# Sliding-window attention and a SwiGLU block on one core: wide half tiles, key spreading on two engines, and another order of the first phase

## The chip, the core and the metric

The kernel runs on one core of a Trainium2 chip. The metric is the device time of one execution in microseconds (us). A profiled execution also gives a span, from its first to its last instruction, which is shorter (in before 405.4 us where the execution took 407.19). PE is TensorE (matmuls), PEld its weight loads, DVE is VectorE, ACT is ScalarE, POOL is GpSimd, and SP is the engine whose queue issues the loads and stores here. A trailing q (SPq, POOLq) means the queue of that engine. One execution of e10 fell into a slower state (584.02 us at a granted clock of 0.643, against 0.959 to 0.966 in its other runs); all comparisons below are of runs in the fast state.

## The reference

```python
# q, k, v: (8 batches, 8 heads, 576 positions, 64)
scores = q @ k.T / 8, kept where 0 <= query position - key position < 64
attn   = softmax(scores)
x      = (attn @ v) laid out as 4608 tokens x 512
out    = (silu(x @ w_gate) * (x @ w_val)) @ w_out      # 512 -> 1536 -> 512
```

## The kernel before

Attention is done in groups of 128 tokens, inputs come in blocks of 256 tokens (number n), and the feed-forward part works on tiles of 512 tokens (number t). All of it is one program: a first phase fills the pipeline, then a loop over groups 8 to 35 mixes attention of later groups with feed-forward of earlier ones. In the timelines below an engine's instructions start in the order in which the program gives them: in the changed kernel ScalarE's query copy starts at 24.32 us, after the key copies that stand ahead of it, though TensorE had turned the queries by 21.0.

Keys of a block are transposed on TensorE into one PSUM tile `tp`, and spread from there into a block-diagonal SBUF tile. Queries are transposed and copied by ScalarE:

```python
    def turn_k(n):
        tp = turned(n, "k_f")                 # 8 transposes into one PSUM tile
        for a in range(2):                    # a: half of the partitions
            for c in range(2):                # c: even or odd keys
                y = 64 * a + c
                dve.tensor_copy(
                    kbd[n % KR][64 * a:64 * a + 64, :, :, y:y + 63:2],
                    tp[64 * a:64 * a + 64, c].rearrange("r p (i x) -> r p i x", x=32),
                )

    def turn_q(n):
        tp = turned(n, "q_f")
        act.copy(qT[n % QR][:], tp[:])
```

The feed-forward step `gv` computes gate and value for one block of 128 channels, over `n` columns from `c0`. In the first phase, where only half a tile of tokens is ready, it takes 256 columns:

```python
        for ps, w in ((g_ps, wg), (v_ps, wv)):
            for c in range(4):
                nc.tensor.matmul(
                    ps[:, 0:n], w[:, c, P * m:P * m + P], xT[t][:, c, c0:c0 + n],
                    start=(c == 0), stop=(c == 3),
                )
        act.activation(th[:, 0:n], g_ps[:, 0:n], AF.Tanh, scale=0.5)
# gate:   sg = (th + 1) * g_ps        value: hT = sg * v_ps        (both on VectorE)
```

`mix(xs, ys)` issues the feed-forward steps xs and deals the attention steps ys out between them. The end of the first phase:

```python
    mix(O(0, (2, 3)), [lambda: products(9), lambda: scores(11, pool), lambda: turn_x(9)])
    casts_all(6, pool, act)
    mix(F(1, range(8, 12), 256, 256),
        [lambda: products(10), lambda: turn_k(6), lambda: turn_q(6), lambda: turn_x(10),
         lambda: scores(12, pool)])
    load(8, k, "k_f", sp)
    load(8, q, "q_f", sp)
    casts(7, "k_f", pool)
    # ... cut: products, scores and turns of the last groups before the loop
    for w in range(8, NG):                    # the loop
        ...
```

The softmax here doesn't subtract the row's maximum and nothing guards it: scores larger than these inputs give would overflow.

## Time and profile before

| | before |
|---|---|
| time, median of 3 runs | 407.66 us (406.01 to 408.82) |
| span of the profiled run | 405.4 us |
| first gate matmul | 20.2 us |
| start of the loop (its first gate matmul) | 117.4 us |
| from there to the end of the span | 288.0 us |
| PE busy from 117.4 to 386.0 | 266.7 of 268.6 us |

The page's digits show in which slices an engine is busy. A table by stage says how full each engine is in a stretch of time, and the list of waits says what a given engine stood for. The lines are in the prediction below. What they say is short: the loop is bound by TensorE and has no waits; the first 117 us have 27.5 us of holes on TensorE, so that is where a change can win.

### The profile page before, as it was taken

To read this page: it belongs to the slowest core of one execution; us is meant where nothing else is said; L and a number is where in the kernel's file an instruction comes from. 1 tells how busy PE (TensorE), PEld (TensorE's weight loads), DVE (VectorE), ACT (ScalarE), POOL (GpSimd) and SP (SyncE) were. 2 spreads that over 40 slices of the span, in tenths; PEclk is the share of its full clock that TensorE was granted. 3 is DMA by queue.
4 is the path that set the end of the run, shared out by engine and by line. 5 is a ranking of instruction groups with operands and counts; after the bars stand their busy time and mean duration, and the time that the engine had idled before them with its cause. 6 is when DMAs were issued, how large, how long until landed. Compare 5 with 4: busy or idle time off the path is not lost.

```text
span 405.4 us, 7092 instructions
## 1 busy us (share of the span) xinstructions
PE 357.0 (88%) x2617; PEld 211.8 (52%) x2656; DVE 248.5 (61%) x511; ACT 170.4 (42%) x307; POOL 152.4 (38%) x194
## 2 busy tenths in 40 slices
PE   2596898989779999999999999999999999999910
PEld 1474657675655555555555555555555554444400
DVE  6777988756667675747576676767676544554100
ACT  3353545363653545344444445343535434322200
POOL 4542333463574445554444445554443420000000
PEclk9998999999989999999999999999999999999975
DMA  9999897036442444434443434444432100111111
GB/s 190 237 220 228 162 199 169 3 119 163 134 105 62 113 108 111 112 106 108 107 112 107 106 108 112 120 124 114 114 76 57 35 32 27 31 39 36 36 52 44
DMA packets 87411, 42.94 MB, mean 106 GB/s; under 512 B 40272, under 2 KB 82768, under 8 KB 87376
## 3 DMA queue, kind: packets, MB, share of 16 engines
q1 hardware_dynamic: 81552, 37.76, 36.5%
q0 software_dynamic: 5824, 4.72, 7.3%
q8 instruction: 21, 0.34, 0.3%
q14 instruction: 14, 0.11, 0.1%
HBM read 37.75 MB, written 9.44 MB: 116 GB/s over the span
## 4 chain that ended last, share of the span: by engine, by line
PE 78%; DVE 8%; DMA 3%; ACT 3%; issue 2%; POOL 1%; SPq 0%; DVEq 0%; ACTq 0%; POOLq 0%
PE g_ps L251 22%; PE v_ps L251 22%; PE o_ps L276 21%; PE ao_ps L220 5%; PE tp L129 4%; DMA out_dram<-os__5021 2%; PE xtp L236 2%; DVE kbd_93 L137 2%; PE s_ps L189 2%; DVE kbd_95 L137 1%; DVE x_b L225 1%; DMA k_f<-in_k_dram 1%; DVE sg L262 1%; DVE hT L267 1%; PE s_ps L182 1%
## 5 line engine op out<-in xcount | busy, mean ns | idle before, releaser
L262 DVE SCALAR_TENSOR_TENSOR sg<-th,g_ps 128x512 f32<-128x512 f32 (+1 forms) x126 | 76.7, 609 | 76.4 <-ACT th L256 74.9
L251 PE MATMUL g_ps<-xT,wg 128*128 128x512 bf16 (+1 forms) x487 | 114.3, 353 | 5.7 <-DVE sg L262 3.0
L251 PE MATMUL v_ps<-xT,wv 128*128 128x512 bf16 (+1 forms) x500 | 115.2, 352 | 0.5
L256 ACT ACTIVATE th<-g_ps 128x512 f32<-128x512 f32 (+1 forms) x126 | 67.9, 539 | 110.1 <-PE g_ps L251 95.4
L276 PE MATMUL o_ps<-wo,hT 128*128 128x512 bf16 x414 | 96.0, 379 | 0.6
L267 DVE TENSOR_TENSOR hT<-sg,v_ps 128x512 bf16<-128x512 f32 (+1 forms) x126 | 76.8, 610 | 11.4 <-PE ao_ps L220 0.5
L251 PEld LDWEIGHTS <-wv 128*128 128x128 bf16 x504 | 50.0, 99 | 45.2
L251 PEld LDWEIGHTS <-wg 128*128 128x128 bf16 x504 | 47.2, 100 | 38.6 <-issue 6.2
L276 PEld LDWEIGHTS <-hT 128*128 128x128 bf16 x432 | 41.2, 98 | 44.6
L225 DVE TENSOR_TENSOR x_b<-ao_ps,r 128x256 bf16<-128x256 f32 x72 | 30.6, 425 | 2.5
L192 POOL TENSOR_TENSOR E_104<-E_104,mask 128x512 bf16<-128x512 bf16 (+1 forms) x16 | 17.6, 1123 | 33.2 <-ACT E_104 L191 29.7
L192 POOL TENSOR_TENSOR E_102<-E_102,mask 128x512 bf16<-128x512 bf16 (+2 forms) x18 | 17.0, 964 | 27.9 <-ACT E_102 L191 27.9
L192 POOL TENSOR_TENSOR E_105<-E_105,mask 128x512 bf16<-128x512 bf16 x16 | 18.1, 1152 | 23.1 <-ACT E_105 L191 23.1
L238 ACT COPY xT<-xtp 128x512 bf16<-128x512 bf16 x36 | 21.3, 591 | 12.8 <-PE xtp L236 12.8
L137 DVE COPY kbd_94<-tp 64x512 bf16<-64x512 bf16 x24 | 16.0, 716 | 11.5 <-PE tp L129 11.4
L137 DVE COPY kbd_95<-tp 64x512 bf16<-64x512 bf16 x24 | 16.0, 715 | 9.9 <-PE tp L129 9.8
L137 DVE COPY kbd_93<-tp 64x512 bf16<-64x512 bf16 x24 | 16.0, 716 | 8.6 <-PE tp L129 8.5
L192 POOL TENSOR_TENSOR E_103<-E_103,mask 128x512 bf16<-128x512 bf16 x14 | 15.8, 1155 | 11.4 <-ACT E_103 L191 11.4
L129 PE MATMUL tp<-identb,k_fb 128*128 128x128 bf16 x144 | 12.3, 234 | 6.9 <-DVE k_fb L100 6.7
L236 PE MATMUL xtp<-identb,x_b 128*128 128x128 bf16 x144 | 14.9, 226 | 1.9 <-DVE x_b L225 1.4
L100 POOL CAST k_fb<-k_f 128x1024 bf16<-128x1024 f32 x15 | 15.5, 1036 | 0.7
L129 PEld LDWEIGHTS <-k_fb 128*128 128x128 bf16 x144 | 10.5, 106 | 9.3 <-DVE k_fb L100 6.7
(148 smaller groups left out, 422.7 us busy)
## 6 DMA issues: line engine op xcount, KB each, us to landing
v_f<-in_v_dram SPq DMA_DIRECT2D x144, 64.0 KB
k_f<-in_k_dram SPq DMA_DIRECT2D x12, 512.0 KB
q_f<-in_q_dram SPq DMA_DIRECT2D x12, 512.0 KB
wg<-in_moe_w_gate_dram POOLq DMA_DIRECT2D x4, 384.0 KB, 6.9
wv<-in_moe_w_val_dram POOLq DMA_DIRECT2D x4, 384.0 KB, 8.8
k_f<-in_k_dram SPq DMA_DIRECT2D x4, 384.0 KB
q_f<-in_q_dram SPq DMA_DIRECT2D x4, 384.0 KB
wo<-in_moe_w_out_dram POOLq DMA_DIRECT2D x4, 384.0 KB, 10.1
```

What stands on the lines that cost most here:

```text
L129: nc.tensor.transpose(tp[:, c, p, :], x_b[:, c, P * p:P * p + P], identb[:])
L137: dve.tensor_copy(kbd[n % KR][64 * a:64 * a + 64, :, :, y:y + 63:2], tp[64 * a:64 * a + 64, c].rearrange("r p (i x) -> r p i x", x=32),)
L192: eng.tensor_mul(e, e, mask[:, lo:hi, :].unsqueeze(1).to_broadcast([P, 2, hi - lo, 64]))
L220: nc.tensor.matmul(o_ps[:, i, :], w, x, start=(n == 0), stop=(n == len(parts) - 1))
L225: dve.tensor_mul(x_b[:, 256 * h:256 * h + 256].rearrange("r (p a d) -> r p a d", p=2, a=2), o_ps[:, :, 0:P].rearrange("r p (a d) -> r p a ...
L236: nc.tensor.transpose(tp[:, p, :], x_b[:, P * p:P * p + P], identb[:])
L238: act.copy(xT[g // 4][:, :, off:off + P], tp[:])
L251: nc.tensor.matmul(ps[:, 0:n], w[:, c, P * m:P * m + P], xT[t][:, c, c0:c0 + n], start=(c == 0), stop=(c == 3),)
L256: act.activation(th[:, 0:n], g_ps[:, 0:n], AF.Tanh, scale=0.5)
L262: dve.scalar_tensor_tensor(sg[:, 0:n], th[:, 0:n], 1.0, g_ps[:, 0:n], ALU.add, ALU.mult)
L267: dve.tensor_mul(hT[t][:, m, c0:c0 + n], sg[:, 0:n], v_ps[:, 0:n])
L276: nc.tensor.matmul(o_ps[:], hT[t][:, c, P * s:P * s + P], wo[:, c, :], start=(c == 0), stop=(c == 11),)
```

## The change

The intent: elementwise work on half tiles takes more than half the time of a full tile (the step for `sg` in before: 416 ns at 256 columns, 686 at 512), so a half tile takes two channel blocks at once and stays 512 wide. VectorE was busy in the holes, so half of the key copies go to ScalarE and many clears to GpSimd. The first phase gets an order in which attention and feed-forward alternate more evenly. Weights come in other slices.

```diff
     def turn_k(n):
         tp = turned(n, "k_f")
-        for a in range(2):
-            for c in range(2):
+        for c in range(2):
+            for a, copy in ((0, dve.tensor_copy), (1, act.copy)):
                 y = 64 * a + c
-                dve.tensor_copy(
+                copy(
                     kbd[n % KR][64 * a:64 * a + 64, :, :, y:y + 63:2],
                     tp[64 * a:64 * a + 64, c].rearrange("r p (i x) -> r p i x", x=32),
                 )
@@ gv: a half tile takes channel blocks m and m + 1
+            for i in range(1 if half is None else 2):
+                o, n, x = (0, 512, 0) if half is None else (256 * i, 256, 256 * half)
+                for c in range(4):
+                    nc.tensor.matmul(
+                        ps[:, o:o + n], w[:, c, P * (m + i):P * (m + i) + P],
+                        xT[t][:, c, x:x + n], start=(c == 0), stop=(c == 3),
+                    )
@@ clears: half of each buffer, values on GpSimd, ahead of their use
+    def clear(i):
+        for a in range(2):
+            ...
+            dve.memset(kbd[i][h, :, :, z:z + 64], 0.0)
+            for vb in vbd[2 * i:2 * i + 2]:
+                pool.memset(vb[h, :, :, z:z + 64], 0.0)
+                ...
@@ inputs of the last blocks
+    def next_inputs(n):
+        casts_all(n, pool, act)
+        load(n + 1, k, "k_f", sp)
+        load(n + 1, q, "q_f", sp)
+        load_v(2 * n + 2)
+        load_v(2 * n + 3)
+
+    def last_inputs():
+        casts(7, "k_f", pool)
+        casts(7, "q_f", act)
+        load(8, k, "k_f", sp)
+        load(8, q, "q_f", sp)
@@ order (cut to its last mixture)
+    mix(F(0, range(8, 12)) + F(1, (0, 2, 4, 6), 1) + O(0, (0, 1)) + F(1, (8, 9)) + O(0, (2, 3))
+        + F(1, (10, 11)), att3[5:] + [
+            lambda: turn_k(4), lambda: turn_q(4), lambda: scores(8, pool, 1, 4),
+            lambda: next_inputs(5), lambda: scores(9, pool), lambda: products(8),
+            lambda: turn_x(8), lambda: turn_k(5), lambda: turn_q(5), lambda: scores(10, pool),
+            lambda: next_inputs(6), lambda: products(9), lambda: scores(11, pool),
+            lambda: turn_x(9), lambda: turn_k(6), lambda: products(10), lambda: turn_q(6),
+            lambda: turn_x(10), lambda: scores(12, pool), last_inputs, lambda: products(11),
+            lambda: scores(13, pool), lambda: turn_x(11), lambda: turn_k(7), lambda: turn_q(7)])
```

More of the change, by code (lines that the diff above doesn't have):

```diff
@@ L152, in queries, with weights_gv @@
         return x[:, m % 4:m % 4 + n]
-    def weights_gv(s):
+    def weights_gv(m0, m1):
         for dst, src in ((wg, moe_w_gate), (wv, moe_w_val)):
             pool.dma_start(
-                dst[:, :, 384 * s:384 * s + 384],
-                src[:, 384 * s:384 * s + 384].rearrange("(c r) f -> r c f", r=P),
+                dst[:, :, P * m0:P * m1],
+                src[:, P * m0:P * m1].rearrange("(c r) f -> r c f", r=P),
             )
@@ L162, in weights_o @@
         pool.dma_start(
-            wo[:, 3 * s:3 * s + 3, :],
-            moe_w_out[384 * s:384 * s + 384].rearrange("(c r) f -> r c f", r=P),
+            wo[:, 6 * s:6 * s + 6, :],
+            moe_w_out[768 * s:768 * s + 768].rearrange("(c r) f -> r c f", r=P),
         )
@@ L241, with gv @@
     parts_gv = {}
-    def gv(t, m, c0=0, n=512):
-        if m == 0 and c0 == 0:
+    def gv(t, m, half=None):
+        if t not in hT:
             hT[t] = hpool.tile([P, 12, 512], BF16, name="hT", tag="hT")
@@ L249, in gv, with gate, value, gate_value @@
         for ps, w in ((g_ps, wg), (v_ps, wv)):
-            for c in range(4):
-                nc.tensor.matmul(
-                    ps[:, 0:n], w[:, c, P * m:P * m + P], xT[t][:, c, c0:c0 + n],
-                    start=(c == 0), stop=(c == 3),
-                )
+            for i in range(1 if half is None else 2):
[5 more added lines that the diff above has]
+                    )
         th = fsb.tile([P, 512], FP32, name="th", tag="th")
-        act.activation(th[:, 0:n], g_ps[:, 0:n], AF.Tanh, scale=0.5)
+        act.activation(th[:], g_ps[:], AF.Tanh, scale=0.5)
         return g_ps, v_ps, th
-    def gate(state, n=512):
+    def gate(state):
         g_ps, v_ps, th = state
         sg = fsb.tile([P, 512], FP32, name="sg", tag="sg")
-        dve.scalar_tensor_tensor(sg[:, 0:n], th[:, 0:n], 1.0, g_ps[:, 0:n], ALU.add, ALU.mult)
+        dve.scalar_tensor_tensor(sg[:], th[:], 1.0, g_ps[:], ALU.add, ALU.mult)
         return v_ps, sg
-    def value(state, t, m, c0=0, n=512):
+    def value(state, t, m, half=None):
         v_ps, sg = state
-        dve.tensor_mul(hT[t][:, m, c0:c0 + n], sg[:, 0:n], v_ps[:, 0:n])
-    def gate_value(t, ms, c0=0, n=512):
-        for m in ms:
-            value(gate(gv(t, m, c0, n), n), t, m, c0, n)
+        if half is None:
+            dve.tensor_mul(hT[t][:, m, :], sg[:], v_ps[:])
+        else:
+            dve.tensor_mul(
+                hT[t][:, m:m + 2, 256 * half:256 * half + 256],
+                sg[:].rearrange("r (m x) -> r m x", m=2), v_ps[:].rearrange("r (m x) -> r m x", m=2),
+            )
+    def gate_value(t, m, half=None):
+        value(gate(gv(t, m, half)), t, m, half)
     def project(t, s, ps, tag):
@@ L299, in casts_all, with F @@
         casts_v(2 * n + 1)
-    def F(t, ms, c0=0, n=512):
-        return [lambda m=m: gate_value(t, (m,), c0, n) for m in ms]
+    def F(t, ms, half=None):
+        return [lambda m=m: gate_value(t, m, half) for m in ms]
     def O(t, ss):
@@ L329, in mix @@
             done = upto
+    def next_inputs(n):
[11 more added lines that the diff above has]
+        for a in range(2):
+            z = 64 - 64 * a
+            h = slice(64 * a, 64 * a + 64)
+            dve.memset(kbd[i][h, :, :, z:z + 64], 0.0)
+            for vb in vbd[2 * i:2 * i + 2]:
+                pool.memset(vb[h, :, :, z:z + 64], 0.0)
+                pool.memset(vb[h, :, :, P + a:P + a + 1], 1.0)
+                pool.memset(vb[h, :, :, P + 1 - a:P + 2 - a], 0.0)
     loads(0)
     dve.memset(mask[:], 1.0)
-    dve.memset(kbd[0][:], 0.0)
-    for vb in vbd[0:2]:
-        dve.memset(vb[:], 0.0)
     for a in range(2):
@@ L347 @@
     make_identity(nc, identb[:])
-    weights_gv(0)
+    weights_gv(0, 2)
     loads(1)
     for E in Es:
-        pool.memset(E[:, 0:21:5, :], 0.0)
-    for vb in vbd[0:2]:
-        for a in range(2):
-            dve.memset(vb[64 * a:64 * a + 64, :, :, P + a:P + a + 1], 1.0)
+        dve.memset(E[:, 0:21:5, :], 0.0)
+    clear(0)
     casts_all(0, dve, act)
-    weights_gv(1)
+    weights_gv(2, 4)
+    clear(1)
     att0, att1 = attention(0, dve), attention(1, dve)
-    for step in att0[:5]:
+    for step in att0:
@@ L359 @@
         step()
     loads(2)
-    for vb in vbd[2:4]:
-        dve.memset(vb[:], 0.0)
-        for a in range(2):
-            dve.memset(vb[64 * a:64 * a + 64, :, :, P + a:P + a + 1], 1.0)
-    dve.memset(kbd[1][:], 0.0)
-    att0[5]()
-    att0[6]()
-    att0[7]()
-    att0[8]()
-    casts_all(1, dve, act)
-    weights_gv(2)
-    mix(F(0, range(0, 3), 0, 256), att1[0:4])
-    dve.memset(kbd[2][:], 0.0)
-    mix(F(0, range(3, 6), 0, 256), att1[4:8])
-    for vb in vbd[4:]:
-        dve.memset(vb[:], 0.0)
-        for a in range(2):
-            dve.memset(vb[64 * a:64 * a + 64, :, :, P + a:P + a + 1], 1.0)
@@ L379 @@
-    att1[8]()
-    weights_gv(3)
-    casts_all(2, dve, act)
+    casts_all(1, pool, act)
+    weights_gv(4, 8)
+    clear(2)
+    mix(F(0, (0,), 0), att1[0:5])
+    att1[5]()
+    att1[6]()
+    casts_all(2, pool, act)
+    weights_gv(8, 12)
+    mix(F(0, (2,), 0), att1[7:])
     loads(3)
-    att2 = attention(2, dve)
-    mix(F(0, range(0, 6), 256, 256), att2[0:4])
+    att2 = attention(2, pool)
+    mix(F(0, (0, 2), 1), att2[0:5])
+    casts_all(3, pool, act)
     weights_o(0)
     weights_o(1)
-    mix(F(0, range(6, 9)), att2[4:8])
@@ L388 @@
-    weights_o(2)
-    weights_o(3)
     loads(4)
-    casts_all(3, pool, act)
+    mix(F(0, range(4, 8)), att2[5:])
+    mix(F(1, (0, 2), 0), [])
     att3 = attention(3, pool)
-    mix(F(0, range(9, 12)), att2[8:])
-    mix(F(1, range(0, 12), 0, 256), att3[0:8])
+    mix(F(1, (4, 6), 0), att3[0:5])
+    casts_all(4, pool, act)
     loads(5)
-    casts_all(4, pool, act)
-    mix(O(0, (0, 1)), att3[8:] + [lambda: turn_k(4), lambda: turn_q(4), lambda: scores(8, pool, 1, 4)])
-    loads(6)
-    mix(F(1, range(0, 4), 256, 256), [lambda: scores(9, pool), lambda: products(8)])
@@ L400 @@
-    casts_all(5, pool, act)
-    mix(F(1, range(4, 8), 256, 256),
-        [lambda: turn_x(8), lambda: turn_k(5), lambda: turn_q(5), lambda: scores(10, pool)])
-    load(7, k, "k_f", sp)
-    load(7, q, "q_f", sp)
-    mix(O(0, (2, 3)), [lambda: products(9), lambda: scores(11, pool), lambda: turn_x(9)])
-    casts_all(6, pool, act)
-    mix(F(1, range(8, 12), 256, 256),
-        [lambda: products(10), lambda: turn_k(6), lambda: turn_q(6), lambda: turn_x(10),
-         lambda: scores(12, pool)])
@@ L410 @@
-    load(8, k, "k_f", sp)
-    load(8, q, "q_f", sp)
-    casts(7, "k_f", pool)
-    casts(7, "q_f", act)
-    load_v(14)
-    load_v(15)
-    products(11)
-    scores(13, pool)
-    turn_x(11)
-    turn_k(7)
-    turn_q(7)
+    mix(F(0, range(8, 12)) + F(1, (0, 2, 4, 6), 1) + O(0, (0, 1)) + F(1, (8, 9)) + O(0, (2, 3))
[7 more added lines that the diff above has]
+            lambda: scores(13, pool), lambda: turn_x(11), lambda: turn_k(7), lambda: turn_q(7)])
@@ L454 @@
             load_v(w + 8)
-        gate_value(t, (3 * s + 2,))
+        gate_value(t, 3 * s + 2)
     for s in range(4):
```

## The prediction

> **What bounds the kernel now.** I read the page's share lines and its 40 slices first, then a table of busy time by stage, then TensorE's waits, then the timeline of the stage that idles.
>
> The share line and two slice lines (one digit is the busy share of 10.1 us, in tenths):
>
> ```profile
> PE 357.0 (88%) x2617; PEld 211.8 (52%) x2656; DVE 248.5 (61%) x511; ACT 170.4 (42%) x307; POOL 152.4 (38%) x194
> ...
> PE   2596898989779999999999999999999999999910
> ...
> DVE  6777988756667675747576676767676544554100
> ```
>
> TensorE is full from about slice 12 to the end and has holes only before it. The stage table (columns: length, then busy us and instruction count of PE, PEld, DVE, ACT, POOL, then granted clock, DMA share, GB/s):
>
> ```profile
> 0.00:20.20 20.20, 7.62 (x60) 5.91 (x61) 14.15 (x35) 6.59 (x12) 9.97 (x24) 1.00 1.09 214
> 20.20:36.80 16.60, 12.96 (x117) 10.11 (x117) 12.71 (x35) 7.41 (x17) 4.56 (x7) 0.98 1.26 211
> 36.80:59.70 22.90, 20.75 (x162) 13.63 (x164) 19.82 (x46) 11.97 (x23) 9.13 (x14) 0.94 1.04 196
> 59.70:75.50 15.80, 14.37 (x161) 12.77 (x161) 12.99 (x33) 7.70 (x19) 7.68 (x11) 1.00 0.57 124
> 75.50:117.40 41.90, 34.16 (x334) 25.43 (x334) 23.94 (x59) 22.44 (x41) 21.39 (x25) 0.97 0.44 121
> 117.40:386.00 268.60, 266.74 (x1790) 144.00 (x1824) 164.88 (x308) 113.65 (x196) 99.67 (x116) 1.00 0.31 84
> ```
>
> The loop over groups 8 to 35 starts at 117.4 us. There PE is busy 266.74 of 268.6 us and the list of its waits is empty, so only the first 117.4 us can shrink. In them PE is busy 89.9 us and idle 27.5, of which 6.75 come before the first transpose. The largest waits of PE there:
>
> ```profile
> PE tp L129 <- DVE k_fb L100: 6.7, 1, 6.7
> PE ao_ps L220 <- DVE x_b L225: 3.5, 2, 2.3
> PE g_ps L251 <- DVE sg L262: 3.0, 3, 1.4
> PE s_ps L189 <- DVE kbd_93 L137: 2.4, 2, 1.4
> PE ao_ps L220 <- POOL E_102 L192: 2.3, 2, 1.7
> PE g_ps L251 <- ACT xT L238: 2.0, 3, 0.7
> ```
>
> VectorE holds the early stages up (12 to 20 us busy of 16 to 23), VectorE and GpSimd the later one. Why x_b is late, from the timeline of VectorE (start, length):
>
> ```profile
> 15.88 0.91 DVE L365 MEMSET kbd_94<- 128x1024 uint32 x1 [0.26 <-issue]
> 16.82 0.18 DVE L224 RECIPROCAL r<-ao_ps 128x4 f32<-128x4 f32 x1
> ```
>
> From 13.9 to 16.8 us VectorE clears buffers for later groups while the first attention result waits. Unit costs, from the groups kept apart by shape (busy, mean ns):
>
> ```profile
> L262 DVE SCALAR_TENSOR_TENSOR sg<-th,g_ps 128x512 f32<-128x512 f32 x90 | 61.7, 686 | 63.0 <-ACT th L256 61.7
> ...
> L137 DVE COPY kbd_94<-tp 64x512 bf16<-64x512 bf16 x24 | 16.0, 716 | 11.5 <-PE tp L129 11.4
> ...
> L262 DVE SCALAR_TENSOR_TENSOR sg<-th,g_ps 128x256 f32<-128x256 f32 x36 | 15.0, 416 | 13.4 <-ACT th L256 13.1
> ```
>
> [...] 416 and 686 ns at 256 and 512 columns are 146 ns fixed and 1.05 ns a column. [...] the first k cast takes 1.68 us, from 5.01, while GpSimd's memsets run until 6.13, and 0.69 at 37.55. [...] after the start and the pause at 36 us a group of four 256-column matmuls takes 0.85 us, else 0.44.
>
> **The change, part by part.**
> *Half tiles.* Before, 36 half steps of 256 columns. A pair costs VectorE 2 x (416 + 421) = 1674 ns; one wide step costs 686 + 687 = 1373. Twelve wide half steps replace 24 narrow ones, and the other twelve become six full tiles, as those come later in the order. So 18 x 0.30 = 5.4 us leave VectorE, and 18 x (2 x 388 - 599) = 3.2 us leave ScalarE. Matmul columns stay the same.
> *Key spreading.* Two of four copies of 0.67 us (spacing in the timeline) move to ScalarE, at some 0.58 us each by its xT copy of 512 columns (estimate). Keys are ready 1.35 us earlier where nothing else binds, but queries then wait: ScalarE does 1.16 us of keys before its 1.01 us query copy. In the loop VectorE loses 0.67 us a group of 9.5 us, ScalarE gains 0.6; PE waits for neither, so I count nothing.
> *Clears.* Half of each key and value buffer is cleared, values on GpSimd, keys and E borders on VectorE, before they are urgent.
> *Order.* I followed each stage by hand with the durations above:
>
> - To the first gate matmul (before 20.23). GpSimd now clears four half value blocks from 4.85; by its 128x256 memset (0.31) and 128x320 (0.38) some 0.5 us each, with small ones 2.4, to 7.2. [...] The two-engine spreading hides some, the query copy ends at 11.2 against 10.2. Masks end at 14.5, x_b follows without the 2.9 us of memsets, xT is ready at 17.8. Start 17.9: **2.3 gained**.
> - Group pair 1 (before: second xT ready, 36.77). One wide step, then attention without filler, then another, cold. I get 33.0, with one pair of half steps less done (1.7 us of PE): gain stays **2.1**.
> - Group pair 2 (before 59.7). Masks go to GpSimd (1.15 us each against 0.42 on VectorE); products wait about 1 us on them. I get 53.4 with two full steps less done (3.4 us): gain **2.9**.
> - Pair 3 and the long mixture (before 117.4): PE work at full speed from 53.4: 14 steps x 1.72 + 4 projections x 2.6 + 5 key/query turns x 0.9 + 6 products x 0.7 + 6 x turns x 0.22 + 9 score groups (4.2) = 24.1 + 10.4 + 4.5 + 4.2 + 1.3 + 4.2 = 48.7 us. Waits I find: 2.3 for score buffers; 1.3 for the masks of group 7; 1.1 twice for queries; 3.6 at the products of group 8, because the new input casts (1.04 + 4 x 0.64 = 3.6 us of GpSimd) stand ahead of group 9's masks; some 1.0 at groups 9 and 11. Sum 10.4 (my stage walk, with overlaps counted once, gives 8.2). The loop starts at 110.3 (walk) to 112.5 (sum), against 117.4.
>
> Gain 4.9 to 7.1 us. I take 6.4, for the walk ignores few latencies and fills are better spread than before: 407.7 - 6.4 = **401.3 us**.
>
> **Rivals.**
> A. *GpSimd becomes the bound.* It gets value clears, two more k casts, pair 2's masks, and casts ahead of masks. For: the 2.3 + 1.4 + 0.6 us for E masks before. Against: only 21.4 of 41.9 us busy in the last stage. If each mask wait doubled, gain 1 to 3: 404.5 to 406.5.
> B. *DMA is the bound to 50 us.* Its share is above 1.0 there. Against: PE never waits on a transfer, first gate weights shrink from 384 to 256 channels, and channels 512 to 1023 are needed near 40 us, some 14 us after their issue by my walk (before, weights landed 5.5 to 11.9 us after issue). If the queries of pair 3 came late, ScalarE would stand at their cast and hold tanh: 1 to 2 us lost, 402 to 404.
> C. *The holes close almost wholly.* [...] the loop then starts near 107: 397 us. For: busy VectorE explained most early holes. Against: the GpSimd order above.
> D. *ScalarE delays the loop.* The ten key turns of the loop add 1.2 us each; its 113.65 of 268.6 us leaves room. Improbable.
>
> **Range and chances.** The centre is 401.3; A and B pull up by 2 to 5, C down by 4, and runs of before span 406.0 to 408.8. So 397.0 to 405.5. 2% is 8.2 us: below 399.5. Only C and part of the central case reach that: 0.30. Slower by 2% would need a new stall of 14 us against my count: 0.03. Within 2%: 0.67.
>
> **What would show it.** Right: first gate matmul near 17.9; no memset on VectorE between the first masks and x_b; the first k cast longer than 2 us; no 256-wide elementwise work on sg, hT and th; kbd copies half on ScalarE at about 0.6 us; waits of PE for sg nearly gone; the largest new wait at the products of group 8, on a GpSimd mask, near 3.6 us; the loop's start near 111 and its length unchanged within 1 us. Wrong: PE waits on weights or q transfers before 60 us; ScalarE's copies above 1 us; or waits in the loop.

## The result

The changed kernel took **428.83 us** (median of 3, 425.31 to 429.03) against 407.66: slower, with a ratio of 1.0496 (95% interval 1.0396 to 1.0597). A ratio here is the mean time of one kernel's fast runs over that of the other's fast runs of the same rounds, so it is not quite the ratio of the medians.

The page of the changed kernel, its shares and the slices of PE, DVE and DMA (10.7 us a slice):

```profile
PE 365.8 (86%) x2608; PEld 209.9 (49%) x2608; DVE 217.6 (51%) x420; ACT 192.4 (45%) x325; POOL 163.5 (38%) x232
...
PE   1756979668895999999999999999999999999930
...
DVE  5654666542444545556556565655545556546100
...
DMA  9999998400514334333344433343332111001111
```

VectorE got its relief: 217.6 us against 248.5. TensorE is no fuller for it: it has holes up to slice 13, and in slices 9 and 10 DMA nearly stands still. The table by stage, with the columns as before:

```profile
0.00:18.24 18.24, 7.21 (x61) 6.16 (x62) 10.92 (x28) 8.07 (x14) 13.44 (x43) 1.00 1.12 210
18.24:34.15 15.91, 10.13 (x101) 8.91 (x101) 9.10 (x21) 8.72 (x15) 8.71 (x22) 0.79 1.23 221
34.15:54.25 20.10, 16.12 (x132) 10.91 (x132) 11.18 (x22) 10.23 (x18) 12.74 (x18) 0.92 1.11 190
54.25:126.00 71.75, 58.09 (x492) 39.22 (x492) 33.75 (x64) 36.16 (x60) 29.11 (x35) 0.93 0.46 95
126.00:415.30 289.30, 274.24 (x1827) 144.68 (x1824) 152.62 (x287) 129.21 (x219) 99.52 (x116) 0.99 0.31 84
```

In stages 2 to 4 no compute engine is full, which is the picture of engines waiting for each other. (The DMA share is 1.12, 1.23 and 1.11 in the first three stages, against 1.09, 1.26 and 1.04 before, but no wait of TensorE for a transfer is listed there.) The loop begins at 126.0 us instead of 117.4, and takes 301.3 us to the end instead of 288.0. So 8.6 us were lost ahead of the loop and 13.3 in it, where the prediction had expected nothing at all. TensorE's largest waits:

```profile
PE s_ps L187 <- ACT qT L144: 14.8, 5, 4.3
PE tp L129 <- DVE k_fb L100: 6.6, 1, 6.6
PE ao_ps L220 <- POOL E L192: 4.2, 3, 3.1
PE tp L129 <- POOL k_fb L100: 3.4, 1, 3.4
PE g_ps L254 <- DVE sg L265: 2.6, 9, 0.3
PE s_ps L189 <- ACT qT L144: 2.5, 1, 2.5
```

The first line is new: scores stand for the query copy of ScalarE, 14.8 us in five waits. What ScalarE did before that copy, from its timeline (start, length, then the idle time before it and what ended it):

```profile
22.08 0.72 ACT L137 COPY kbd<-tp 64x512 bf16<-64x512 bf16 x1 [2.17 <-DVE kbd L137]
23.58 0.72 ACT L137 COPY kbd<-tp 64x512 bf16<-64x512 bf16 x1 [0.78 <-DVE kbd L137]
24.32 1.01 ACT L144 COPY qT<-tp 128x1024 bf16<-128x1024 bf16 x1
```

The same turn on VectorE:

```profile
21.34 0.71 DVE L137 COPY kbd<-tp 64x512 bf16<-64x512 bf16 x1
22.83 0.71 DVE L137 COPY kbd<-tp 64x512 bf16<-64x512 bf16 x1 [0.78 <-ACT kbd L137]
```

In the kernel before, VectorE makes its four copies in a row, and ScalarE's query copy runs beside them (a turn of the first stage):

```profile
7.82 2.68 DVE L137 COPY kbd_93<-tp 64x512 bf16<-64x512 bf16 x4 [1.13 <-PE tp L129]
9.19 1.01 ACT L144 COPY qT_106<-tp 128x1024 bf16<-128x1024 bf16 x1 [1.13 <-PE tp L129]
```

In the changed kernel the four copies never overlap: VectorE at 21.34, ScalarE at 22.08, VectorE at 22.83, ScalarE at 23.58. Each waits for the one before. The spreading takes 3.0 us, more than the 2.7 of VectorE alone, and ScalarE is held all the while: TensorE had turned the queries by 21.0 us, but their copy comes after the key copies on ScalarE and starts at 24.32. In the whole run ScalarE stood idle 36.6 us for VectorE's copies:

```profile
ACT kbd L137 <- DVE kbd L137: 36.6, 36, 4.2
```

A second thing is at the loop's start. The eighth k block is wanted by GpSimd as soon as the loop begins:

```profile
138.30 1.03 POOL L100 CAST k_fb<-k_f 128x1024 bf16<-128x1024 f32 x1 [10.57 <-DMA k_f<-in_k_dram]
```

Its issue on the SP queue, in the changed kernel:

```profile
120.88 4.84 SPq L292 DMA_DIRECT2D out_dram<-os__1527  x2
125.82 2.24 SPq L84 DMA_DIRECT2D k_f<-in_k_dram  x1
```

and in the kernel before:

```profile
103.37 1.76 SPq L84 DMA_DIRECT2D k_f<-in_k_dram  x1
```

The new order puts `load(8)` into `last_inputs`, which comes after the last two projections; in the queue the load follows their stores (issued at 118.42 and 120.88 us; with the load ahead of them in the program, e4 below, it was issued at 117.80). It is issued 0.2 us before the loop starts, where the kernel before issued it 14 us ahead.

Two theories follow. **T1, lock step:** the two engines copy the keys one after the other, which delays the queries and everything behind them on ScalarE. **T2, late load:** the order of the first phase makes the loop begin on a stall. A rival to T1, **T1b**, is that ScalarE's added work hurts, with or without a wait.

### The profile page after: what moved, and what is told of

It is laid out like the page before. It is cut to its first block, busy times and chain, and to the rows that moved or that the text cites. A ratio compares the mean times of both kernels' runs of the same rounds, so it can differ in the third digit from the quotient of the medians.

```text
span 427.3 us, 6969 instructions
## 1 busy us (share of the span) xinstructions
PE 365.8 (86%) x2608; PEld 209.9 (49%) x2608; DVE 217.6 (51%) x420; ACT 192.4 (45%) x325; POOL 163.5 (38%) x232
## 4 chain that ended last, share of the span: by engine, by line
PE 56%; DVE 16%; ACT 11%; DMA 6%; POOL 4%; issue 3%; SPq 0%; DVEq 0%; POOLq 0%; ACTq 0%
PE o_ps L284 19%; PE g_ps L254 14%; PE v_ps L254 13%; DVE kbd L137 5%; ACT kbd L137 5%; DVE sg L265 4%; DMA k_f<-in_k_dram 4%; PE ao_ps L220 4%; DVE x_b L225 3%; POOL E L192 3%; ACT th L259 3%; PE tp L129 2%; DVE hT L271 2%; DMA out_dram<-os__4866 2%; PE xtp L236 2%
## 5 line engine op out<-in xcount | busy, mean ns | idle before, releaser
L265 DVE SCALAR_TENSOR_TENSOR sg<-th,g_ps 128x512 f32<-128x512 f32 x108 | 74.1, 686 | 109.1 <-ACT th L259 108.0
L192 POOL TENSOR_TENSOR E<-E,mask 128x512 bf16<-128x512 bf16 (+2 forms) x70 | 73.3, 1069 | 121.7 <-ACT E L191 116.7
L259 ACT ACTIVATE th<-g_ps 128x512 f32<-128x512 f32 x108 | 63.8, 599 | 86.0 <-PE g_ps L254 83.9
L271 DVE TENSOR_TENSOR hT<-sg,v_ps 128x512 bf16<-128x512 f32 x96 | 65.8, 685 | 7.9 <-DVE sg L265 0.5
L118 POOL CAST vbd<-v_f 64x512 bf16<-64x512 f32 x72 | 43.9, 609 | 57.0 <-DMA v_f<-in_v_dram 54.7
L137 DVE COPY kbd<-tp 64x512 bf16<-64x512 bf16 x36 | 25.8, 717 | 41.5 <-PE tp L129 27.3
L191 ACT ACTIVATE E<-s_ps 128x512 bf16<-128x512 f32 (+3 forms) x82 | 39.4, 545 | 14.7 <-PE s_ps L189 14.2
L137 ACT COPY kbd<-tp 64x512 bf16<-64x512 bf16 x36 | 26.0, 722 | 36.6 <-DVE kbd L137 36.6
L220 PE MATMUL ao_ps<-vbd,E 128*128 128x130 bf16 x428 | 33.4, 230 | 6.5 <-POOL E L192 4.2
L220 PEld LDWEIGHTS <-E 128*128 128x128 bf16 x428 | 29.1, 103 | 15.4 <-POOL E L192 5.1
L238 ACT COPY xT<-xtp 128x512 bf16<-128x512 bf16 x36 | 21.1, 590 | 7.3 <-PE xtp L236 7.2
L187 PE MATMUL s_ps<-qT,kbd 128*128 128x64 bf16 x68 | 9.3, 199 | 14.8 <-ACT qT L144 14.8
```

Of the source, the lines that this page charges most:

```text
L118: pool.tensor_copy(vbd[g % VR][64 * a:64 * a + 64, :, :, 64 * a:64 * a + 64], v_f[64 * a:64 * a + 64],)
L137: copy(kbd[n % KR][64 * a:64 * a + 64, :, :, y:y + 63:2], tp[64 * a:64 * a + 64, c].rearrange("r p (i x) -> r p i x", x=32),)
L191: act.activation(e, s_ps[:, :, lo:hi, :], AF.Exp, scale=0.125)
L192: eng.tensor_mul(e, e, mask[:, lo:hi, :].unsqueeze(1).to_broadcast([P, 2, hi - lo, 64]))
L220: nc.tensor.matmul(o_ps[:, i, :], w, x, start=(n == 0), stop=(n == len(parts) - 1))
L259: act.activation(th[:], g_ps[:], AF.Tanh, scale=0.5)
```

## The experiments

Eleven kernels ran; all gave correct results. The runs e1 to e4, e5 to e8, and e9 to e11 share a chip and their runs of before; between these parts the ratio to before is the safer comparison. "Loop at" is the first gate matmul of the loop in the profiled run, "loop" the time from there to the end of its span; both are of a single execution.

| run | edit | median us | ratio to before | loop at | loop |
|---|---|---|---|---|---|
| before | | 407.66 | | 117.4 | 288.0 |
| after | | 428.83 | 1.0496 | 126.0 | 301.3 |
| e1_keys_vector | after, keys on VectorE | 415.17 | 1.0186 | 117.6 | 296.8 |
| e2_two_banks | after, split over two PSUM tiles | 414.18 | 1.0148 | 115.1 | 297.4 |
| e3_before_split | before, with the change's split | 425.00 | 1.0421 | 126.7 | 297.2 |
| e4_load8_early | after, load 8 earlier | 425.20 | 1.0416 | 125.9 | 297.9 |
| e5_banks_load8 | e2 and e4 together | 404.22 | 0.9910 | 114.2 | 288.0 |
| e6_masks_first | e5, masks ahead of casts | 398.82 | 0.9777 | 107.7 | 288.1 |
| e7_before_banks | before, split over two PSUM tiles | 403.64 | 0.9904 | 114.1 | 287.7 |
| e8_before_wide | before, wide half steps only | 404.13 | 0.9916 | 115.5 | 288.2 |
| e9_e6_keys_vector | e6, keys on VectorE | 403.59 | 0.9895 | 113.6 | 288.4 |
| e10_e6_one_bank | e6, both engines on one PSUM tile | 419.94 | 1.0316 | 119.8 | 298.0 |
| e11_e6_three_to_one | e6, three copies to one | 399.55 | 0.9795 | 108.0 | 287.9 |

The median of before in the three later parts was 407.48, 407.62 and 407.62 us. One run of e10 took 584 us at a clock of 0.643; it is in the slow state and left out of the median and the ratio (with it the median is 420.35).

**e1_keys_vector**

```diff
-        for c in range(2):
-            for a, copy in ((0, dve.tensor_copy), (1, act.copy)):
+        for a in range(2):
+            for c in range(2):
                 y = 64 * a + c
-                copy(
+                dve.tensor_copy(
```

> The changed kernel with all four key copies back on VectorE, everything else changed. T1 (the two engines copy the keys in lock step, 3.0 us a turn instead of 1.4, and ScalarE's later work stands behind it) expects most of the loss back: 403 to 413 us, TensorE's waits for the queries (17.3 us in all after) below 8 us, and no wait for sg in the loop (2.6 us after). T2 (the eighth input load stands behind the outputs, so that the loop starts on a stall; the new order is what costs) expects 418 us or more, with the 10.6 us wait of GpSimd for the k transfer still there. If both act, 410 to 418.

Measured: 415.17 us, 13.7 less than after (428.83). That is above the range of T1 alone and within the range for both theories. TensorE's waits for queries fell from 17.3 to 3.3 us (waits for the keys themselves rose to 7.1), and its wait for sg is gone. But its wait for the k cast grew from 3.4 to 6.1 us: an earlier loop runs into the same late load. Both theories act.

**e2_two_banks**

```diff
-        tp = turned(n, "k_f")
-        for c in range(2):
-            for a, copy in ((0, dve.tensor_copy), (1, act.copy)):
+        x_b = cast_qk.pop(("k_f", n))
+        for c, copy in ((0, dve.tensor_copy), (1, act.copy)):
+            tp = ps_a.tile([P, 4, P], BF16, name="tk", tag="a")     # a PSUM tile for each engine
+            for p in range(4):
+                nc.tensor.transpose(tp[:, p, :], x_b[:, c, P * p:P * p + P], identb[:])
+            for a in range(2):
                 y = 64 * a + c
                 copy(kbd[...][64 * a:64 * a + 64, :, :, y:y + 63:2], tp[64 * a:64 * a + 64]...)
```

> The changed kernel with the split kept, but each engine has its own PSUM tile to read (VectorE the even keys, ScalarE the odd ones), so that no engine waits for the other between copies. T1 expects the spreading to take about 1.5 us, the idle time of ScalarE before its key copies to fall from 36.6 us to under 10, and 400 to 410 us. T1b (not the lock step but ScalarE's extra 1.4 us a turn is what hurts) expects no more than 4 us off the 428 of after.

Measured: 414.18 us; as in e1, above T1's range because of the late load. The key copies run side by side now. ScalarE, then VectorE, in their timelines of this run:

```profile
21.63 1.47 ACT L140 COPY kbd<-tk 64x512 bf16<-64x512 bf16 x2 [1.96 <-PE tk L137]
23.12 1.01 ACT L147 COPY qT<-tp 128x1024 bf16<-128x1024 bf16 x1
```

```profile
21.38 1.46 DVE L140 COPY kbd<-tk 64x512 bf16<-64x512 bf16 x2
```

ScalarE no longer waits for VectorE here. The idle time before its key copies is 11.5 us, a little more than the 10 expected; it waits for TensorE, in one case for 7.3 us behind the late load:

```profile
ACT kbd L140 <- PE tk L137: 11.5, 6, 7.3
PE tk L137 <- POOL k_fb L100: 6.9, 1, 6.9
```

ScalarE has exactly as many key copies as in after, 36 of 0.72 us, and the kernel is 14.7 us faster. That rules out T1b: not the work hurt, but the waiting. What is left is the wait for k, which is now larger, 6.9 us on TensorE (the second line above), and the loop is 9.4 us longer than that of before.

**e3_before_split**

```diff
-        for a in range(2):
-            for c in range(2):
+        for c in range(2):
+            for a, copy in ((0, dve.tensor_copy), (1, act.copy)):
```

> The kernel before with nothing but the split key spreading of the change (lock step). T1 expects it clearly slower than before: 412 to 425 us, with TensorE waiting for queries and a loop some 4 to 6 us longer than 288. T2 expects 406 to 411, as the order of loads is that of before.

Measured: 425.00 us, at the upper end of T1's range. The split alone, in the old order, costs 17.5 us: by the spans some 9.3 ahead of the loop and 9.2 in it, where T1 had expected 4 to 6. T1 holds, its cost in the loop was underrated, and the loss in the loop is not a matter of order.

**e4_load8_early**

```diff
     def next_inputs(n):
         ...
         load_v(2 * n + 3)
+        if n == 6:
+            load(8, k, "k_f", sp)
+            load(8, q, "q_f", sp)
     def last_inputs():
         ...
-        load(8, k, "k_f", sp)
-        load(8, q, "q_f", sp)
```

> The changed kernel with the loads of the eighth k and q issued right after the seventh's v, ahead of the last outputs of the first tile, and nothing else. T1 alone expects 422 to 427 (the 3.4 us wait of TensorE for k and some slow clock after it go). T2 expects under 415.

Measured: 425.20 us, within what T1 alone expected. GpSimd no longer waits for k, and the loop is 3.4 us shorter than that of after. The late load costs little here and more in e2; probably because the lock step makes the loop slow anyway, which no run tests by itself. So the two causes cannot simply be added.

**e5_banks_load8** (the edits of e2 and e4 together)

> The changed kernel with both faults mended: each engine has its own PSUM tile for the keys, and the eighth k and q are loaded early. T1 and T2 together expect the sum and more, because the 6.9 us stall and the slow clock after it go whole: 403 to 407 us, no wait of TensorE above 0.5 us after the loop has begun. If the loss has a third cause (the order or the clears themselves), it stays at 409 or more.

Measured: 404.22 us, ratio 0.991. The loop takes 288.0 us, the same as before, and begins at 114.2. Mending two faults took 24.6 us off 428.83, of which e2 alone takes 14.7 and e4 alone 3.6: each hides part of the other. No third cause of the loss is left.

**e6_masks_first**

```diff
-            lambda: next_inputs(5), lambda: scores(9, pool), lambda: products(8),
+            lambda: scores(9, pool), lambda: next_inputs(5), lambda: products(8),
```

> e5 with one swap: the masks of group 9 ahead of the casts of the next inputs on GpSimd. The prediction's step of the group 8 products (3.6 us reckoned, 3.1 + 0.6 us measured in after) expects 2.5 to 4 us less than e5: 400 to 404. If the time merely moves to the next wait (the casts then come late), less than 1 us.

Measured: 398.82 us, 5.4 less than e5 and more than expected. TensorE's wait for GpSimd's masks in e5:

```profile
PE ao_ps L223 <- POOL E L195: 5.4, 5, 3.1
```

and in e6:

```profile
PE ao_ps L223 <- POOL E L195: 2.3, 4, 0.6
```

The wait of 3.1 us is gone whole. More is won in the matmuls right after the pause. In e5:

```profile
82.14 1.91 PE L257 MATMUL g_ps<-xT,wg 128*128 128x256 bf16 x8
```

and in e6:

```profile
77.11 1.04 PE L257 MATMUL g_ps<-xT,wg 128*128 128x256 bf16 x8
```

In e5 the gate and value matmuls of this step run at about half speed (granted clock 0.70 from 80 to 85 us): they last until 85.48 us, 3.3 us in all, where those of e6 last until 78.86, 1.75 in all, at a clock of 1.00 from 75 to 80 us. So with the pause go its own 3.1 us and 1.6 us of a slow TensorE behind it. The profiled loops begin 6.5 us apart, but 1.7 of that is not the edit's: the last gate matmuls that come before the swap are already at 75.58 us in e5 and 73.84 in e6, though the programs are the same up to there (more on this under e9). Against before e6 is faster, ratio 0.9777 (0.9743 to 0.9810): it beats both kernels, though whether by more than 2% is not certain.

**e7_before_banks** (the kernel before, with the `turn_k` of e2)

> The kernel before with the key spreading split over two PSUM tiles (no lock step), nothing else. T1 expects no loss at all and a little gain, from the key copies that scores wait for (2.4 + 0.6 us) and the sg waits behind them (2.8 us): 402 to 407 us. If ScalarE's added work is itself harmful, 409 to 415.

Measured: 403.64 us, ratio 0.9904. The split is a small gain in the old order as soon as the two engines do not share a PSUM tile. Between e3 and e7 lie 21.4 us, for one PSUM tile more or less (and for dealing the keys out by even and odd instead of by halves of the partitions, which e10 tests apart).

**e8_before_wide** (the kernel before, with `gv`, `gate` and `value` of the change, and its half steps taken in pairs)

```diff
-    mix(F(0, range(0, 3), 0, 256), att1[0:4])
+    mix(F(0, (0, 2), 0), att1[0:4])
-    mix(F(1, range(0, 12), 0, 256), att3[0:8])
+    mix(F(1, (0, 2, 4, 6, 8, 10), 0), att3[0:8])
   ... the other half steps likewise
```

> The kernel before with the wide half steps (two channel blocks of 256 columns) and nothing else: order, clears and keys as before. The prediction's part 1 (5.4 us off VectorE, 3.2 off ScalarE, a part of them on the path) expects 402 to 407. Fewer and larger pieces to interleave could cost as much: 407 to 410.

Measured: 404.13 us, ratio 0.9916: a gain of 3.5 us, in the range expected. The loop is unchanged and begins 1.9 us earlier in the profiled run.

**e9_e6_keys_vector** (e6 with the `turn_k` of before)

> e6 with all four key copies on VectorE from one PSUM tile. It asks what an honest split is worth in this order. After a turn the queries' scores need both keys and queries: two banks give VectorE 1.44 us and ScalarE 1.44 + 1.01 us, VectorE alone 2.7 us. So little is expected: the same as e6 or up to 2 us more, 399 to 401. If the split is what carries e6's gain, 403 or more.

Measured: 403.59 us, 4.8 more than e6. The likely range was missed, and the other branch came true: the split over two PSUM tiles carries much of what e6 gains. TensorE's waits for keys and queries are 9.1 us in e9 and 6.7 in e6, which is 2.4 of the 5.9 us by which e9's loop begins later. The first gate matmuls show another piece. In e9:

```profile
17.16 1.87 PE L254 MATMUL g_ps<-xT,wg 128*128 128x256 bf16 x8 [0.67 <-ACT xT L238]
```

and in e6:

```profile
17.03 1.03 PE L257 MATMUL g_ps<-xT,wg 128*128 128x256 bf16 x8 [0.67 <-ACT xT L241]
```

The same eight matmuls run at half speed in e9, and with the eight after them this sets e9 back by 1.6 us. It need not be an effect of the keys: e5 has the split of e6 and the same program up to the swap, and in its profiled run it was 1.7 us behind e6 there (75.58 against 73.84 us). So executions of the same instructions can differ by as much. Some 1.9 of the 5.9 us are left without an account, and how much of the 4.8 us in the medians is the start is open. (That TensorE was slow is read from the spacing of the matmuls. Their granted clock does not always show it: in before four gate matmuls at 20.23 us took 0.81 us to the next group, against 0.43 at 41.56, and the clock from 20 to 26 us was 1.00.)

**e10_e6_one_bank**

```diff
-        x_b = cast_qk.pop(("k_f", n))
-        for c, copy in ((0, dve.tensor_copy), (1, act.copy)):
-            tp = ps_a.tile([P, 4, P], BF16, name="tk", tag="a")
-            ...
+        tp = turned(n, "k_f")                                      # one PSUM tile again
+        for a in range(2):
+            for c, copy in ((0, dve.tensor_copy), (1, act.copy)):
                 y = 64 * a + c
                 copy(kbd[...][64 * a:64 * a + 64, :, :, y:y + 63:2], tp[64 * a:64 * a + 64, c]...)
```

> e6 with the same split by parity (VectorE the even keys, ScalarE the odd ones), but both engines read one PSUM tile again. It separates the shared tile from the way in which the copies are dealt out. If the shared PSUM tile makes the lock step, 415 to 424 with some 30 us of ScalarE idle before its key copies; if the dealing-out by halves of the partitions did, 399 as e6.

Measured: 419.94 us over its five fast runs, 21.1 more than e6. ScalarE deals with the same keys as in e6, writes the same SBUF tile, and waits again:

```profile
ACT kbd L137 <- DVE kbd L137: 33.8, 36, 2.2
```

So the lock step comes with the shared PSUM tile, and not from dealing the keys out by halves of the partitions, nor from both engines writing `kbd`. The built program, which can be read without a run, says the same. Here are the waits of the key copies in the changed kernel as built, ScalarE's two copies (first line) and VectorE's two (second and third):

```
TensorCopy kbd_93<-tp 64x16x32 [waits DVE_49] x2
TensorCopy kbd_93<-tp 64x16x32 [waits PE_49]
TensorCopy kbd_93<-tp 64x16x32 [waits Activation_49]
```

In e2 the first copy of each engine waits for PE alone, and the second for nothing. So the waits between the engines come with the one PSUM tile. Whether they are needed for a right result was not shown: no version with one tile and without these waits was run.

**e11_e6_three_to_one**

```diff
     # ... cut: both PSUM tiles are filled first, then:
+        for c, a, copy in ((0, 0, dve.tensor_copy), (1, 1, act.copy), (0, 1, dve.tensor_copy), (1, 0, dve.tensor_copy)):
```

> e6 with three key copies on VectorE and one on ScalarE, two PSUM tiles; the ScalarE copy goes first in its tile, so VectorE need not wait for it. Keys would be ready at 2.15 us and queries at 1.73 instead of 2.45: 0.3 us less at each of some five waits for the queries: 396.5 to 398.5. Within noise of e6 would not surprise.

Measured: 399.55 us, the same as e6 within the scatter of both (397.6 to 400.9, and 396.8 to 399.6). Waits for queries fell from 6.4 to 4.7 us, and waits for keys rose from 0.3 to 3.3. The balance of the two engines is not worth more here.

## Why the prediction was wrong

**The step that failed is the one on key spreading.** It said "Keys are ready 1.35 us earlier where nothing else binds" and, for the loop, "PE waits for neither, so I count nothing". It took the two engines' copies to run at the same time, which was the author's estimate and not shown by the trace of before. In its place the runs show four copies in turn, 3.0 us instead of 1.35, with ScalarE held for all of it (and its copies took 0.72 us each, where 0.58 had been estimated). By the profiled runs of pairs that differ only in the key copies this costs 11.7 us (e4 against e5) or 12.1 (e10 against e6) ahead of the loop, and 9.9 in it. The built program's waits could have been read before predicting; only the order of its instructions was.

**Rival D was rejected for a wrong reason.** "ScalarE delays the loop" was judged by ScalarE's load, 113.65 of 268.6 us. It was not load but standing still in order: in the changed kernel's loop ScalarE waited 20.5 us for VectorE's copies, so tanh came late, and VectorE and TensorE waited for it. (The waits of TensorE that the profile lists there, apart from the one for k, come to 5.9 us; the rest of the 9.9 was not itemised.) Busy time says nothing of that.

**Rival B was rejected for a wrong reason too.** It looked for late transfers before 60 us and in the bandwidth. The late one came at 126 us, by its place in the queue. Load 8 issued behind four stores cost 3.4 us in the loop with the lock step (after against e4), and 9.4 us without it (e2 against e5): a 6.9 us wait, and then TensorE at half speed (the four gate matmuls at 130.66 us took 1.91 us, against 1.03 at 115.14 us).

**The group 8 wait was right.** "3.6 at the products of group 8, because the new input casts ... stand ahead of group 9's masks": measured 3.1 and 0.6 us at 88 us in after, and worth 5.4 us when removed (e6).

**The first stage was nearly right.** The first gate matmul was foreseen at 17.9 us; it came at 18.2 in after and at 17.0 in e6 without the lock step. Within it one step was wrong: the first k cast was to take longer than 2 us. It took 1.48 us and ended at 6.6, while GpSimd's memsets ran from 4.85 to 7.7 us.

**Wide half steps were right in kind.** They alone gain 0.84% (e8), about 3.5 of the 8.6 us that they were reckoned to take off two engines.

**The walk as a whole.** Its first stages seem to hold even in after: the third and fourth stage begin at 34.2 and 54.3 us, foreseen at 33.0 and 53.4. That is partly luck: without the lock step and with a fast start (e6) they begin at 31.4 and 49.1, so the walk was too slow there by about as much as the lock step, which it left out, costs. The miss shows in the last stage, 71.8 us instead of 56.9. The walk put the loop's start at 110.3 us with the group 8 wait. With both faults mended it is 114.2 (e5, which was 1.7 us behind e6 ahead of the swap), and 107.7 without the wait (e6); the loop is unchanged, as foreseen. The predicted 401.3 us stands between these two kernels, 404.2 and 398.8, but that does not make it right: the kernel that was asked about contained both faults.

**What stays open.** Why the eighth k block needs 12.5 us from issue (125.82) to use (138.30) in after, where the first block, the first load of its queue, was in use 4.3 us after its issue (0.81 to 5.11). Also why the first eight gate matmuls took 1.87 us in e9 and 1.03 in e6.

## What to carry to other kernels

When work on one PSUM tile is split between two engines, give each engine a tile of its own, and read the waits of the built program, not only the order of its instructions: here one tile more was worth 21 us of 400. Waits put into an engine's stream delay what stands behind them, and its busy share does not say whether it has room: in the changed kernel's loop ScalarE was busy 129.2 of 289.3 us and stood 20.5 us for VectorE's copies. When an order is changed, follow each load's place in its queue against the stores that have come ahead of it, up to the point where the first consumer asks for it.

## What the traces showed beside the question

- Two engines on one PSUM tile, as built, took turns at 0.75 us each, a 3.0 us chain (after) instead of 1.46 (e2), and it cost 21.1 us of the kernel (e10 against e6).
- A series of memsets on GpSimd did not hold VectorE up for its whole length: in after the k cast took 1.48 us, from 5.11, beside 2.9 us of memsets, and the one of these memsets that began at 6.08 us took 0.97 us, where the three others of its shape took 0.52 to 0.55.
- A contiguous ScalarE copy of 128x512 took 0.59 us, but the key copies of 64x512, which write every second element, took 0.72 (e2 and after); the two differ in partitions as well as in the step.
- Two pauses of TensorE were followed by slow matmuls: in e6 one of 2.13 us ended at 21.96, eight gate matmuls at 26.87 us took 1.91 us against 1.03 at 31.35, and the granted clock was 0.78 from 17.2 to 33.0 us; in e5 one of 3.12 us ended at 80.72, eight gate matmuls at 82.14 us took 1.91 us against 1.04 at 86.15, and the clock was 0.70 from 80 to 85 us.
